# Attention, a gated MLP and a mixer block on one core: two weight chunks and one output-weight slab move between the first batch's v products

## The chip, the cores and the metric

The kernel runs on one core of one Trainium2 chip. The core has five engines that work side by side: TensorE (PE, matrix products), VectorE (DVE), ScalarE (ACT), GpSimd (POOL) and SyncE (SP), which here issues nearly all DMAs. Each engine works through its own instructions in order and waits on semaphores for the others. The metric is the device time of one execution in microseconds; the time of the kernel is the median of its runs.

## The reference

Four batches of 576 tokens, model width 512. Three blocks follow one another, all in float32:

```python
# 1. attention, 8 heads of 64, rotary embedding on q and k
attn = softmax(rotate(q) @ rotate(k).T / 8) @ v          # -> x [4, 576, 512]
# 2. spatial gating
h = gelu_tanh(x @ w_in);  u, v = h[..., :512], h[..., 512:]
v_n = (v - mean(v)) / sqrt(var(v) + 1e-6) * g_ln          # over the 512 features
v_s = einsum('ts,bsd->btd', w_sg, v_n) + b_sg             # over the 576 tokens
x = x + (u * v_s) @ w_out
# 3. mixer: low rank over the tokens (rank 32), then a channel MLP 512 -> 2048 -> 512
u = x + (x.transpose(0, 2, 1) @ U @ V).transpose(0, 2, 1)
out = u + maximum(u @ w_ch1, 0) @ w_ch2
```

The weights come in as 64-bit floats: they are loaded as pairs of 32-bit words, and the kernel makes 32-bit floats of them with integer steps on the chip.

## The kernel before, in words

The kernel has three stages. Attention (0 to about 295 us in the profile) is written out by hand. The gating stage (about 295 to 540) runs batch by batch, and the channel stage (from about 540) computes the last MLP for all tokens, with combined weight blocks.

In the gating stage the order on PE is the order of the code. On DVE, ACT, POOL and SP the program's planner places the instructions when the kernel is built, by readiness in its own model and by the order of the code; once placed, each engine keeps its order. `tc.issue_after(x)` holds the instructions traced inside it behind `x` on `x`'s engine.

The parts for a batch `b`, each float32 product made of products of high and low parts:

- `v_step(b, t)`: the v product of 128 tokens. At the end of a group of one or two `t`: GELU on ACT, mean and variance on DVE (L634, L635), epsilon added on POOL (L636), power -0.5 on POOL (L637), a small step on DVE (L640), the scaling on ACT (L641), and the high and low parts VH (ACT, L643) and VL (POOL, through `less`, L541). The last group, `t = 4`, holds the tails of two batches; its low parts are made on DVE (L648, L651), and L651 is marked in `LAST_D`.
- `u_step(b, k0)`: the u product with its GELU.
- `s_step(b, d)`: the product over the tokens (tile `m`) with the gate: L672 and L673 on DVE, then the parts GH (ACT) and GL (POOL). Four of them make a batch; the DVE gate L673 is marked in `LAST_G` and `LAST_D`.
- `o_step(b, e)`: the product with the output weights WOH and WOL (tile `w`), added to X on DVE (L691).
- `y_step`, `z_step`, `h_step`: the low rank mixer, with transposes, YH and YL (L712, L718), Z (L731, L732) and a last add to X (L740).
- `x_split(b)`: the parts XH (ACT, L429) and XL (POOL, L432) of the next batch.

PSUM holds four product tiles in rotation, so a product waits until the tile of the fourth before it has been read.

Beside this run the weights. `first_weights` makes 26 chunks of the channel stage's weights, one for each call of `chunk()`. A chunk is one ACT step (L775) and four DVE steps (L771 to L774) on 128x512; every second chunk adds four combine steps on DVE (L782 to L785) and a DMA of the result. It is traced inside `issue_after` for both entries of `LAST_D`, the last marked instruction on DVE and on ACT, as far as there are any. A call also issues the load of the next chunk, into one of two buffers. `other_weights` makes one slab of `w_out` for each `next(ow)`, four in all: an ACT step (L85), four DVE steps (L86 to L89), WOH on ACT (L573) and WOL on POOL. Chunks and slabs share the two buffers `cb`.

Before the change, batch 0 begins with its five v steps and four u steps; chunks 0 and 1 are called after the second and the fourth u step, when `LAST_D` holds L651. The first slab and `x_split(1)` are called behind `LASTS`, which are the last low parts of v on POOL (L644) and DVE (L648) and the last VH on ACT. The other three slabs follow the gates of batch 0, each behind its `LAST_G`.

Of the kernel before, what the change touches and what calls it, by code (L numbers as in the profile page):

```python
# [14 lines left out]
ALU = mybir.AluOpType  # L15
# [51 lines left out]
def tile_kernel(ctx: ExitStack, tc: tile.TileContext, qk, vv, tabs, w_in, g_ln, wsgT, b_sg, w_out, u_r, v_r, w1, w2, out):  # L67
    nc = tc.nc

    def f(ap):  # L70
        return ap.bitcast(F32)
# [8 lines left out]
    def from_f64(t, raw, clamp=nc.vector):  # L80

        lo, hi = raw[:, :, 0], raw[:, :, 1]
        tu = t.bitcast(U32)
        return (
            lambda: nc.scalar.activation(t, hi.bitcast(F32), AF.Abs),  # L85
            lambda: clamp.tensor_scalar(t, t, F64_LEAST, F64_MOST, ALU.max, ALU.min),  # L86
            lambda: nc.vector.tensor_scalar(tu, tu, 5, 2, ALU.logical_shift_left, ALU.logical_shift_right),
            lambda: nc.vector.scalar_tensor_tensor(tu, hi, 0xC0000000, tu, ALU.bitwise_and, ALU.bitwise_or),
            lambda: nc.vector.scalar_tensor_tensor(tu, lo, 29, tu, ALU.logical_shift_right, ALU.bitwise_or),  # L89
        )  # L90
# [326 lines left out]
    for h in range(2, NH):  # L417
        t = NC * h
# [104 lines left out]
    def ps_tile(name):  # L523
        return ps2.tile([P, 2, 512], F32, tag="ps", name=name)
# [15 lines left out]
    def less(out, a, b):  # L540
        return nc.gpsimd.tensor_tensor(out, a, b, ALU.subtract)  # L541
# [7 lines left out]
    def mark(x):  # L549
        LAST_D[0] = x  # L550
        return x
# [13 lines left out]
    def other_weights():  # L565
        for k in range(KT):
            tag = ("YH", "YL")[k % 2]
            raw = py.tile([P, 512, 2], U32, tag=tag, name=tag, bufs=2)
            t = p2.tile([P, 7, 256], F32, tag="cb", name="cb", bufs=2).rearrange("p a b -> p (a b)")[:, :512]
            nc.sync.dma_start(raw.rearrange("p n w -> p (n w)"), w_out[k * P:(k + 1) * P])  # L570
            for fn in from_f64(t, raw):
                fn()
            nc.scalar.activation(WOH[:, k], t, AF.Copy)  # L573
            less(WOL[:, k], t, f(WOH[:, k]))
            yield

    def gelu(t, ps):

        LAST_D[1] = nc.scalar.activation(t, ps, AF.Gelu_apprx_tanh)
        return t  # L580

    def mm3(ps, pairs, halves, first=True, last=True):
        n = len(pairs)
        for j, (l, r) in enumerate(pairs):
            for a in range(halves):
                rr = r[:, a * HALF:(a + 1) * HALF] if halves == 2 else r
                o = ps[:, a, :HALF] if halves == 2 else ps
                nc.tensor.matmul(o, l, rr, start=(first and j == 0), stop=(last and j == n - 1))  # L588

    def x_split(b):  # L590
        for k in range(KT):
            x_hi(b, k)
            x_lo(b, k)
# [15 lines left out]
    def v_step(b, t):  # L609

        if t == NC - 1 and b % 2:
            return
        pp = P
        first, last = next(g for g in (VG0 if b == 0 else VG) if g[0] <= t <= g[1])
        if t == first:
            VP[b] = ps_tile(f"v{b}_{t}")
        ps = VP[b]
        pr = []
        for k in range(KT):
            xh, xl = (TAILS[0][:, k], TAILS[1][:, k]) if t == NC - 1 else (x[:, k, t * P:(t + 1) * P] for x in (XH, XL))  # L620
            pr += [(xh, WVH[:, k]), (xh, WVL[:, k]), (xl, WVH[:, k])]
        mm3(ps[:pp, t - first, :], pr, 1)
        if t < last:
            return
        nt = last - first + 1
        slot[0] = 1024 - slot[0]
        hv = ug.rearrange("p a b -> p (a b)")[:, slot[0]:slot[0] + 1024].rearrange("p (a b) -> p a b", a=2)
        hv = (hv if b else py.tile([P, 2, DF], F32, tag="YL", name="YL", bufs=2))[:, :nt]
        gelu(hv, ps[:pp, :nt])
        st = p2.tile([P, 2, 6], F32, tag="bst", name="bst", bufs=2)  # L630
        mv = p2.tile([P, 2, 2], F32, tag="bmv", name="bmv", bufs=2)
        rs = p2.tile([P, 2], F32, tag="brs", name="brs", bufs=2)
        for j in range(nt):
            nc.vector.bn_stats(st[:pp, j], hv[:, j])  # L634
            nc.vector.bn_aggr(mv[:pp, j], st[:pp, j])  # L635
        nc.gpsimd.tensor_scalar(rs[:pp, :nt], mv[:pp, :nt, 1], 1e-6, None, ALU.add)  # L636
        nc.gpsimd.tensor_tensor(rs[:pp, :nt], rs[:pp, :nt], mhalf[:pp, :nt], ALU.pow)  # L637
        for j in range(nt):
            t = first + j
            nc.vector.scalar_tensor_tensor(mv[:pp, j, 1:], mv[:pp, j, :1], -1.0, rs[:pp, j:j + 1], ALU.mult, ALU.mult)  # L640
            nc.scalar.activation(hv[:, j], hv[:, j], AF.Identity, bias=mv[:pp, j, 1:], scale=rs[:pp, j:j + 1])  # L641
            if t < NC - 1:
                LASTS[2] = nc.scalar.activation(VH[:, t], hv[:, j], AF.Copy)  # L643
                LASTS[0] = less(VL[:, t], hv[:, j], f(VH[:, t]))  # L644
            else:
                a, z = hv[:D, j], hv[D:, j]
                LASTS[2] = nc.scalar.activation(VH[:D, t], a, AF.Copy)
                LASTS[1] = nc.vector.tensor_tensor(VH[D:, t], a, f(VH[:D, t]), ALU.subtract)  # L648
                nc.scalar.activation(VT[D:], z, AF.Copy)
                nc.scalar.activation(VT[:D], z, AF.Copy)  # L650
                mark(nc.vector.tensor_tensor(VT[D:], z, f(VT[D:]), ALU.subtract))  # L651

    def u_step(b, k0):
        ps = ps_tile(f"u{b}_{k0}")
        pr = []
        for k in range(KT):
            wh, wl = WUH[:, k, k0 * P:(k0 + 1) * P], WUL[:, k, k0 * P:(k0 + 1) * P]
            pr += [(wh, XH[:, k]), (wh, XL[:, k]), (wl, XH[:, k])]
        mm3(ps, pr, 2)
        LAST_D[1] = nc.scalar.activation(h2(ug[:, k0]), ps[:, :, :HALF], AF.Gelu_apprx_tanh)  # L660
# [456 lines left out]
    fw = first_weights()  # L1117
    next(fw)
    chunk = lambda: next(fw, None)
    for t in range(NC):  # L1120
        v_step(0, t)
    RB[NP - 1] = p2.tile([P, S], F32, tag="g", name="g", bufs=2)
    for t in sorted(due):
        for fn in due.pop(t):
            fn()
    for k0 in range(KT):
        u_step(0, k0)
        if k0 % 2:
            chunk()
    ow = other_weights()  # L1130
    with ExitStack() as es:
        for x in LASTS:
            es.enter_context(tc.issue_after(x.ins))
        next(ow)
        x_split(1)
    for b in range(B - 1):
        n = b + 1
        for d in range(KT):
            if d == 1 and n > 1:
                x_split(n)  # L1140
            s_step(b, d)
            if b == 0:
                with ExitStack() as es:
                    es.enter_context(tc.issue_after(LAST_G[0].ins))
                    next(ow, None)
            if b == 1:
                if d < 2:
                    run(h_step, b - 1, 2 * d, 2 * d + 1)
                if d % 2:
                    chunk()  # L1150
            if b == 2 and d % 2 == 0:
                chunk()
        run(v_step, n, 0, 1)
        chunk()
        if b == 0:
            run(v_step, n, 2, 3)
            chunk()
        for e in range(2):
            o_step(b, e, 0, KT - 1)
        chunk()  # L1160
        for e in range(2):
            o_step(b, e, KT - 1)
        o_step(b, 2)
        chunk()
        o_step(b, 3)
        if b > 0:
            if n % 2 == 0:
                x_tail(n)
            v_step(n, 2)
            chunk()  # L1170
            run(v_step, n, 3, 4)
            if n == 3:
                chunk()
        if n == 1:
            u_step(n, 0)
            chunk()
            u_step(n, 1)
            run(y_step, b, 0, 2)
            u_step(n, 2)
            run(z_step, b, *range(NC - 1))  # L1180
            y_step(b, 4)
            u_step(n, 3)
            z_step(b, 4)
            chunk()
        elif n == 2:
            run(y_step, b, 0, 2)
            u_step(n, 0)
            chunk()
            run(z_step, b, *range(NC - 1))
            y_step(b, 4)  # L1190
            u_step(n, 1)
            z_step(b, 4)
            u_step(n, 2)
            chunk()
            run(h_step, b, 0, 1)
            u_step(n, 3)
            run(h_step, b, 2, 3)
        else:
            for k0 in range(KT):
                u_step(n, k0)  # L1200
                if k0 % 2:
                    chunk()
    a, b = B - 2, B - 1
# [103 lines left out]
```

## Time and profile before

| what | value |
|---|---|
| median of 3 runs | 914.27 us (913.6 to 918.02) |
| the profiled execution | 912.03 us, of which its span is 910.2 us |
| PE busy | 885.3 us (97% of the span) |
| DVE busy | 738.8 us (81%) |
| ACT busy | 464.7 us (51%) |
| POOL busy | 401.9 us (44%) |
| mean granted clock of PE | 0.996 |

Busy times come from one profiled execution. The span runs from the first to the last instruction; the execution's time lies around it. A view by stretch gives the busy time of each engine in a window; a timeline gives single instructions with the idle time before them and what ended it, in square brackets; a view of waits sums the idle time of an engine by what ended it. In section 4 of the page, the chain that ended last is PE for 65% of the span and DVE for 21%.

### The profile page before, as it was taken

How to read it: one execution, taken by the hardware profiler on the slowest of the kernel's cores; microseconds unless marked ns; L12 is line 12 of the kernel's file. 1: busy time of each engine (PE TensorE's matmuls, PEld its weight loads, DVE VectorE, ACT ScalarE, POOL GpSimd, SP SyncE). 2: the span in 40 equal slices, each digit the busy share in tenths (PEclk: the TensorE clock that was granted, in tenths of full speed). 3: DMA queues.
4: the chain of work that ended last, by engine and by line, in shares of the span. 5: the costliest groups of instructions: out<-in, count | busy, mean ns of one | idle time of the engine just before them, and what ended most of it. 6: DMA issues, size and time to landing. Idle time of an engine off the chain costs nothing.

```text
span 910.2 us, 14331 instructions
## 1 busy us (share of the span) xinstructions
PE 885.3 (97%) x5279; PEld 802.9 (88%) x5279; DVE 738.8 (81%) x991; ACT 464.7 (51%) x719; POOL 401.9 (44%) x302
## 2 busy tenths in 40 slices
PE   8999999999999998889999999999999999999998
PEld 4677878878877897789999988999999999999997
DVE  6677798898998487889799897789889876897557
ACT  4556666666667454433624356554655455544222
POOL 6997778778727455242443333442100110141010
PEclk9999999999999999999999999999999999999999
DMA  6788777687662531525245348968589378647821
GB/s 192 206 193 203 186 203 190 166 213 187 152 170 63 158 107 51 174 86 174 89 150 175 99 143 278 317 240 299 197 277 397 141 247 299 239 126 247 296 86 70
DMA packets 101330, 170.36 MB, mean 187 GB/s; under 512 B 32822, under 2 KB 50508, under 8 KB 101260
## 3 DMA queue, kind: packets, MB, share of 16 engines
q1 hardware_dynamic: 100960, 169.36, 60.3%
q8 instruction: 42, 0.69, 0.3%
q14 instruction: 28, 0.23, 0.1%
q10 hardware_dynamic: 300, 0.08, 0.0%
HBM read 110.07 MB, written 41.49 MB: 167 GB/s over the span
## 4 chain that ended last, share of the span: by engine, by line
PE 65%; DVE 21%; DMA 4%; ACT 4%; issue 4%; POOL 2%; SPq 0%; DVEq 0%; POOLq 0%; ACTq 0%
PE pv L278 12%; PE st L251 8%; PE sm L209 4%; DVE cb L773 2%; PE v L588 2%; PE w L588 1%; PE u L588 1%; DVE cb L774 1%; DVE cb L771 1%; DVE MX L214 1%; PE m L588 1%; DVE cb L772 1%; PE a2X L907 1%; PE r2x L907 1%; PE a4X L907 1%
## 5 line engine op out<-in xcount | busy, mean ns | idle before, releaser
L214 DVE TENSOR_REDUCE MX<-sm 128x1 f32<-128x576 f32 (+1 forms) x160 | 117.0, 747 | 36.4 <-PE sm L209 31.1
L278 PE MATMUL pv<-pc,VV 128*65 128x288 f32 (+1 forms) x516 | 145.7, 405 | 0.0
L251 PE MATMUL st<-Q,K 65*128 65x288 f32 (+3 forms) x640 | 126.3, 320 | 2.1 <-ACT pc L254 0.8
L251 PEld LDWEIGHTS st<-Q,K 65*128 65x128 f32 (+3 forms) x640 | 95.0, 178 | 16.7 <-DVE MX L214 1.8
L254 ACT ACTIVATE pc<-st 128x576 f32<-128x576 f32 x129 | 83.1, 645 | 31.0 <-PE st L251 28.6
L278 PEld LDWEIGHTS pv<-pc,VV 128*65 128x65 f32 (+1 forms) x516 | 69.3, 136 | 29.1 <-issue 0.2
L831 POOL TENSOR_TENSOR r1l<-t,r1h 128x768 fp32r<-128x768 f32 x12 | 23.0, 1915 | 156.5 <-ACT r1h L828 140.6
L831 POOL TENSOR_TENSOR r7l<-tmp,r7h 128x768 fp32r<-128x768 f32 x12 | 25.6, 2130 | 116.9 <-ACT r7h L828 85.8
L209 PE MATMUL sm<-K,Q 128*128 128x288 f32 (+1 forms) x320 | 72.0, 315 | 2.1 <-ACT pc L254 0.6
L173 POOL TENSOR_TENSOR Q<-raw,Q 128x576 fp32r<-128x576 f32 x30 | 45.7, 1523 | 29.6 <-ACT Q L168 29.5
L209 PEld LDWEIGHTS sm<-K,Q 128*128 128x128 f32 (+1 forms) x320 | 50.0, 178 | 8.5 <-DVE MX L214 1.3
L154 POOL TENSOR_TENSOR raw<-raw,tab 128x576 f32<-128x576 f32 x31 | 50.6, 1631 | 2.4 <-DMA raw<-in_qk 2.4
L588 PE MATMUL u<-XH,setA 128*128 128x288 f32 x256 | 47.2, 302 | 1.9 <-DVE X L691 1.9
L331 DVE TENSOR_TENSOR X<-stage,rb 64x576 f32<-64x576 f32 x30 | 47.5, 1586 | 1.5 <-DMA rb<-rr 1.0
L156 POOL TENSOR_TENSOR raw<-raw 128x576 f32<-128x576 f32 x31 | 47.6, 1536 | 0.5
L541 POOL TENSOR_TENSOR GL<-g,GH 128x576 fp32r<-128x576 f32 x16 | 26.3, 1651 | 45.6 <-ACT GH L674 45.6
L155 POOL TENSOR_TENSOR raw<-raw,tab 128x576 f32<-128x576 f32 x31 | 44.4, 1433 | 0.0
L588 PEld LDWEIGHTS u<-XH,setA 128*128 128x128 f32 x256 | 39.2, 194 | 2.3 <-DVE X L691 2.1
L588 PE MATMUL v<-setA,XH 128*128 128x512 f32 x128 | 39.6, 391 | 0.0
L294 ACT ACTIVATE stage<-pv 65x576 f32<-65x576 f32 x31 | 20.0, 647 | 29.7 <-PE pv L278 29.6
L775 ACT ACTIVATE cb<-raw 128x512 f32<-128x512 f32 x26 | 17.4, 671 | 34.3 <-DMA raw<-in_w 28.8
L258 ACT ACTIVATE pt<-st 64x576 f32<-64x576 f32 x31 | 19.9, 643 | 27.7 <-PE st L251 27.6
(1149 smaller groups left out, 2494.4 us busy)
## 6 DMA issues: line engine op xcount, KB each, us to landing
raw<-in_qk SPq DMA_DIRECT2D x31, 576.0 KB
combo<-cb SPq DMA_DIRECT2D x16, 896.0 KB
YH<-combo SPq DMA_DIRECT2D x27, 512.0 KB
raw<-in_w SPq DMA_DIRECT2D x26, 512.0 KB
K<-Q SPq DMA_DIRECT2D x30, 288.0 KB
YL<-combo SPq DMA_DIRECT2D x15, 512.0 KB
u<-setA SPq DMA_DIRECT2D x16, 384.0 KB
w2l<-lows SPq DMA_DIRECT2D x12, 512.0 KB
```

Source lines behind the costliest of these rows:

```text
L154: lambda: e.tensor_tensor(raw[:, 0], raw[:, 0], tab[:, 0], ALU.mult),
L155: lambda: e.tensor_tensor(raw[:, 1], raw[:, 1], tab[:, 1], ALU.mult),
L156: lambda: e.tensor_tensor(raw[:, 0], raw[:, 0], raw[:, 1], ALU.add),
L173: nc.gpsimd.tensor_tensor(Q2[:, :S], rot, f(Q1), ALU.subtract)
L209: nc.tensor.matmul(ps[:TS[t], n, :HALF], Q1[:, t * P:t * P + TS[t]], K1[:, n * HALF:(n + 1) * HALF], start=True, stop=True)
L214: nc.vector.tensor_reduce(MXs[h % 2][:TS[t], t:t + 1], ps[:TS[t], :, :HALF], AX.XY, ALU.max)
L251: nc.tensor.matmul(ps[:kk, n, :HALF], l[:, c * P:c * P + kk], r[:, ns], start=st, stop=not st)
L254: nc.scalar.activation(h2(pc[:kk]), ps[:kk, :, :HALF], AF.Exp, scale=0.125)
L278: nc.tensor.matmul(o, l, r, start=(c == 0 and j == 0), stop=(c == NC - 1 and j == len(pr) - 1))
L331: nc.vector.tensor_tensor(X[b][rows, pr], STAGE.pop(h - 1 + a)[:D], RB[i][:, a], ALU.mult)
L588: nc.tensor.matmul(o, l, rr, start=(first and j == 0), stop=(last and j == n - 1))
L831: return e.tensor_tensor(out, a, b, ALU.subtract)
```

## The change

Chunks 0 and 1 are called between the v steps of batch 0, after `t = 1` and `t = 3`. The first slab of `w_out` is called after the first u step, without a hold. Batch 0 calls two chunks behind its gates `d = 1` and `d = 3`, and no longer one after `o_step(b, 2)` and one after `z_step(b, 4)`. Batch 1 calls three chunks at its gates in place of two. Batch 3's only call finds no chunk left. The epsilon of the variance is added on DVE.

```diff
@@ -633,7 +633,7 @@
         for j in range(nt):
             nc.vector.bn_stats(st[:pp, j], hv[:, j])
             nc.vector.bn_aggr(mv[:pp, j], st[:pp, j])
-        nc.gpsimd.tensor_scalar(rs[:pp, :nt], mv[:pp, :nt, 1], 1e-6, None, ALU.add)
+        nc.vector.tensor_scalar(rs[:pp, :nt], mv[:pp, :nt, 1], 1e-6, None, ALU.add)
         nc.gpsimd.tensor_tensor(rs[:pp, :nt], rs[:pp, :nt], mhalf[:pp, :nt], ALU.pow)
         for j in range(nt):
             t = first + j
@@ -1117,21 +1117,22 @@
     fw = first_weights()
     next(fw)
     chunk = lambda: next(fw, None)
+    ow = other_weights()
     for t in range(NC):
         v_step(0, t)
+        if t in (1, 3):
+            chunk()
     RB[NP - 1] = p2.tile([P, S], F32, tag="g", name="g", bufs=2)
     for t in sorted(due):
         for fn in due.pop(t):
             fn()
     for k0 in range(KT):
         u_step(0, k0)
-        if k0 % 2:
-            chunk()
-    ow = other_weights()
+        if k0 == 0:
+            next(ow)
     with ExitStack() as es:
         for x in LASTS:
             es.enter_context(tc.issue_after(x.ins))
-        next(ow)
         x_split(1)
     for b in range(B - 1):
         n = b + 1
@@ -1143,10 +1144,12 @@
                 with ExitStack() as es:
                     es.enter_context(tc.issue_after(LAST_G[0].ins))
                     next(ow, None)
+                if d % 2:
+                    chunk()
             if b == 1:
                 if d < 2:
                     run(h_step, b - 1, 2 * d, 2 * d + 1)
-                if d % 2:
+                if d > 0:
                     chunk()
             if b == 2 and d % 2 == 0:
                 chunk()
@@ -1161,7 +1164,8 @@
         for e in range(2):
             o_step(b, e, KT - 1)
         o_step(b, 2)
-        chunk()
+        if b > 0:
+            chunk()
         o_step(b, 3)
         if b > 0:
             if n % 2 == 0:
@@ -1181,7 +1185,6 @@
             y_step(b, 4)
             u_step(n, 3)
             z_step(b, 4)
-            chunk()
         elif n == 2:
             run(y_step, b, 0, 2)
             u_step(n, 0)
```

## Rows read from the trace of the kernel before

**Rows 1.** Busy time by stretch: window, length, busy time per engine (instructions), clock, DMA.
```profile
305.00:323.00 18.00, 18.00 (x124) 17.15 (x123) 5.00 (x15) 12.00 (x19) 11.26 (x14) 1.00 0.56 166
348.00:396.00 48.00, 39.28 (x256) 36.93 (x256) 36.80 (x61) 21.56 (x35) 20.95 (x18) 0.93 0.29 94
396.00:448.00 52.00, 52.00 (x347) 49.01 (x346) 45.43 (x81) 20.85 (x31) 14.92 (x14) 1.00 0.45 145
448.00:522.00 74.00, 74.00 (x520) 71.65 (x520) 66.56 (x103) 28.61 (x42) 31.06 (x21) 1.00 0.41 132
```

**Rows 2.** Waits of PE, 348 to 396: total us, times, longest.
```profile
PE q L588 <- DVE Z L732: 2.5, 1, 2.5
PE u L588 <- DVE X L691: 1.9, 1, 1.9
PE z L728 <- DVE YL L718: 1.5, 1, 1.5
PE w L588 <- ACT WOH L573: 1.1, 1, 1.1
PE w L588 <- ACT ug L579: 0.9, 1, 0.9
PE w L588 <- POOL WOL L541: 0.8, 1, 0.8
```

**Rows 3.** Timeline of PE behind the first waits: start, length, instruction.
```profile
353.26 0.69 PE L588 MATMUL w<-GH,WOH 128*128 128x288 f32 x2
...
356.31 0.42 PE L588 MATMUL w<-GH,WOL 128*128 128x288 f32 x2
```

**Rows 4.** Timeline of DVE, 318 to 428.
```profile
318.13 0.16 DVE L640 SCALAR_TENSOR_TENSOR bmv<-bmv,brs 128x1 f32<-128x1 f32 x1 [0.99 <-POOL brs L637]
322.46 0.69 DVE L648 TENSOR_TENSOR VH<-YL,VH 64x512 fp32r<-64x512 f32 x1 [4.17 <-ACT VH L647]
...
323.89 0.43 DVE L771 TENSOR_SCALAR cb<-cb 128x512 f32<-128x512 f32 x1
...
326.09 1.93 DVE L88 SCALAR_TENSOR_TENSOR cb<-YH,cb 128x512 uint32<-128x512 uint32 x1
...
336.18 0.82 DVE L672 SCALAR_TENSOR_TENSOR g<-m,small,bh 128x576 f32<-128x576 f32 x1
...
338.70 0.43 DVE L785 TENSOR_TENSOR cb<-cb 128x256 f32<-128x256 f32 x1
...
343.07 0.69 DVE L89 SCALAR_TENSOR_TENSOR cb<-YL,cb 128x512 uint32<-128x512 uint32 x1
...
392.59 1.77 DVE L773 SCALAR_TENSOR_TENSOR cb<-raw,cb 128x512 uint32<-128x512 uint32 x1
394.38 0.69 DVE L732 TENSOR_TENSOR Z<-z,Z 32x512 fp32r<-32x512 f32 x1
...
427.62 0.75 DVE L691 TENSOR_TENSOR X<-w,X 128x576 f32<-128x576 f32 x1
```

**Rows 5.** Timeline of PE at two places that read DVE's results.
```profile
325.26 0.69 PE L588 MATMUL m<-WST,VH 128*128 128x288 f32 x4
325.80 0.56 PE L588 MATMUL m<-WS,VH 128*128 128x288 f32 x3
...
434.03 0.38 PE L710 MATMUL t<-ident,X 128*128 128x128 f32 x2
```

**Rows 6.** Timeline of GpSimd, 315 to 333.
```profile
315.76 0.23 POOL L636 TENSOR_SCALAR brs<-bmv 128x2 f32<-128x2 f32 x1 [0.88 <-DVE bmv L635]
...
325.63 7.35 POOL L432 TENSOR_TENSOR XL<-X,XH 128x576 fp32r<-128x576 f32 x4 [3.41 <-ACT XH L429]
```

**Rows 7.** Busy time while the first weights land, columns as in rows 1.
```profile
305.00:310.00 5.00, 5.00 (x25) 4.15 (x24) 1.03 (x3) 3.08 (x5) 4.07 (x6) 1.00 0.99 291
```

**Rows 8.** Waits of PE, 522 to 570.
```profile
PE w L588 <- POOL GL L541: 0.9, 1, 0.9
PE z L728 <- DVE YH L714: 0.7, 1, 0.7
```

## Prediction

> **What bounds the kernel now.** I read the busy time by stretch first [rows 1]. TensorE (PE) works without a gap from 396 to 522 us, but in 348 to 396 it works 39.28 of 48 us, so 8.7 us are idle, and the mean granted clock is 0.93. The same view shows the odd thing: in 305 to 323 VectorE (DVE) is busy for 5.00 of 18 us, in 348 to 396 for 36.80 of 48. So DVE is nearly empty just before the stretch in which PE starves, and full in it. The waits of PE name the releasers [rows 2]: 1.1 and 0.8 us for a slab of the output weights (WOH, WOL), 0.9 for the GELU that frees a product's PSUM tile, 1.9 for a residual add (X L691), 1.5 for YL, 2.5 for Z; together 8.7. The clock: after the first waits a pair of matmuls takes 0.69 us, later 0.42 [rows 3]. A mean of 0.93 over 48 us, with levels of 1.2 and 2.4 GHz, means 6.7 us at the lower one, which costs at most 3.4 us of work; by the pairs it is 6.7 x (0.69 - 0.42) / 0.69 = 2.6. I take 3.0. So the stretch holds 8.7 + 3.0 = 11.7 us to be had.
>
> Then the order on DVE [rows 4]. The last small step of batch 0's v chain is at 318.13; after it DVE waits 4.17 us for ScalarE, makes the low parts of v's tail (L648 is the first), and at 323.89 the first weight chunk begins. From there to 339.13 stand chunks c0 and c1, the first output slab and, in their midst, one gate (L672 at 336.18, 0.82, with its product about 1.6 together). That is 15.2 - 1.6 = 13.6 us of weights, while the first gate's products were done on PE at 325.8, when the next gate's begin [rows 5]. All that PE waits for after 348 comes behind this on DVE. The chunks start at 323.89 because the code holds their DVE steps behind the last DVE instruction marked before them, the last low part of the v tail, and the output slab stands behind the same low parts.
>
> **Part 1, two chunks between the v products.** At the new place (after v steps 1 and 3) no DVE instruction has been marked yet, so only a GELU on ScalarE holds them. They are 4 + 4 conversion steps and 4 combine steps. Undisturbed, a conversion's two one-input steps take 0.43 each, its two two-input steps 0.69 each (L89 at 343.07), a combine step 0.43 (L785) [rows 4]: 2.24 a conversion. c0, c1 and the slab are 3 x 2.24 + 4 x 0.43 = 8.4 us undisturbed; in the trace they took 13.6, as L88 shows: 1.93 beside the XL work of GpSimd, 7.35 us long [rows 4, 6].
>
> How much idle time can they use? Not all 13.0 of the 18 us: their weights come first. The DMA engines are full (0.99, 291 GB/s) from 305 to 310 [rows 7], and up to the end of the first chunk there are 1.4 MB to land by the tiles' sizes, so by an estimate it is there at 305 + 1.4 / 0.29 = 309.8 us. From then to 323.9 are 14.1 us; DVE uses 5.00 - 1.03 = 4.0 of them [rows 1, 7] and about 0.7 for L648: 9.4 us are free for 8.4. It fits if undisturbed.
>
> **Part 2, the output slab,** behind the first u product: its four DVE steps are in that sum; two ScalarE steps and the low part on GpSimd move too. ScalarE is busy 12.00 of 18 us there and GpSimd 11.26 [rows 1]: room in both, at no cost while the v chain has the room named below. SP issues no more than before: the loads are the same, those of chunks 2 and 3 start earlier as their buffers come free earlier, behind the loads of w_out that were issued with the first.
>
> The rule that speaks against it: measured, a two-input step takes 1.93 us beside GpSimd and 0.69 without [rows 4]. The Trainium skill, GPSIMD Engine Reference, section Specifications, says that GpSimd shares its SBUF interfaces with VectorE, with contention for instructions of two inputs and in two-port modes. The trace agrees; by that rule the moved steps are stretched again wherever GpSimd works, 63% of the time there, and stretch the low parts of v in turn: 8.4 + 0.63 x (13.6 - 8.4) = 11.7 us, more than the 9.4 free.
>
> What PE would notice: L648 ends at 323.15, and PE comes to the matmuls that read it at 325.26 [rows 4, 5]: 2.1 us of room. The moved steps stand in one line with the chain on DVE. Bounds of the chain's delay: 0 (all in gaps) and 13.6 - 9.4 + one long step of 1.93 = 6.1. Less the room, PE waits 0 to 4.0 us, plus up to 1.5 for a fallen clock (half of the 3.0 above). I take +1.0, near the row without contention. Below zero it can't go: PE does not wait here now.
>
> **Part 3, behind the gates.** Chunks 2 and 3 now stand behind the second and the fourth gate of batch 0; the two later ones (after o step 2 and behind z) go. The batch keeps six chunks and loses the 13.6 us of parts 1 and 2. So DVE comes to the last slabs up to 13.6 us earlier, where PE wants them 2 us earlier: the waits of 1.1 and 0.8 go. The gates free the GELU's buffer earlier by the same: the 0.9 goes. X L691 (1.9) has less before it: gone. The Z step at 394.38 stands behind a step of 1.77 of a chunk, at 392.59 [rows 4], and that is the chunk taken from there: the 2.5 goes. YL's 1.5 is partly a chain of its own, two copies on ScalarE and two steps on DVE against one u product: I leave 0.5 of it, and 0.5 for the rest. With the clock back, -11.7 + 1.0 = -10.7; bounds -11.7, and -4.5 if only the first three waits (2.8) and 1.7 of the clock go.
>
> Batch 1 gets one chunk more at its gates, 2.2 us alone and up to 4 x 1.93 = 7.7 beside GpSimd. The next that PE needs behind it are the transposes at 434.03; the residual add that they read begins at 427.62 and takes 0.75 [rows 4, 5]: 5.7 us of room. I take 0, by the row without contention; bounds 0 and +2. Batch 2 keeps nine chunks. Batch 3 loses its only one, 2.24 + 4 x 0.43 = 4.0 us between its gates, and PE waits there 0.9 for GL and 0.7 for YH [rows 8]: bounds 0 and -1.6; I take -0.8, the middle.
>
> **Part 4, epsilon on VectorE.** Eleven adds of 0.23 leave GpSimd [rows 6]; the nearest row of DVE is L640 with 0.16 [rows 4]. Each chain is 0.07 shorter, or longer by up to 1.93 if a moved step comes between. PE waits for no v chain but by the 0.9 above, so I count 0, with +0.16 x 11 = 1.8 of DVE time as the upper bound.
>
> **Sum**, against the profiled execution's own 912.03 us (span 910.2 and 1.8 around it): +1.0 - 10.7 + 0 - 0.8 + 0 = -10.5. The median of the runs, 914.27, is 2.2 above that execution; I set the difference against the median: 903.8, say **904**.
>
> **The rivals.** (a) Half of it: only what hangs on the slabs and gates goes (-4.5); X, Z and YL are late by chains of their own. 914.3 - 4.5 = 909.8. For: Z and YL pass three engines. Against: a chunk's step stands right ahead of Z on DVE [rows 4].
> (b) Slower: the idle time cannot be used, as DVE works its line in order. It is idle while its next instruction waits for GpSimd or ScalarE (4.17 us at L648); if the moved steps wait at the head of that line for their weights, or stand ahead of the chain's, the low part is late by up to 13.6: PE waits 13.6 - 2.1 = 11.5 at 325 and runs slowly after it, 13.0 with the 1.5. DVE is then no longer behind after 348, which gives back 4.5 to 11.7: from +1.3 to +8.5, the middle +4.9: 919.2. It decides from a delay of 5 us on if 4.5 comes back, of 12 if all does. For: full DMA to 310. Against: 9.4 us free for 8.4.
> (c) It does not do what it says: the planner may place the chunks behind the chain all the same. 914. Against: what kept them back is the hold, and that falls.
>
> **How the numbers follow.** Forecast 0.58 (900 to 907.5, or below), (a) 0.20 (907.5 to 912), (b) 0.15, (c) 0.07. A measurement of this kernel tells 0.5%, or 4.6 us, from no change: 909.7 to 918.8 is the same. Half of (a) is faster, half the same; (b) is slower with 0.11, the same with 0.04; (c) the same. So faster 0.68, same 0.21, slower 0.11. The range leaves out 0.13 above, most of (b), and 0.07 below 900, where all the bounds fall well: 900 to 914.5.
>
> **What would show it.** Right: L771 to L774 and L782 to L785 on DVE before 323; the first gate (L672) near 326 instead of 336; no wait of PE above 0.5 us in what is now 348 to 396, with a clock near 1.00; the same work of PE behind it, about 10 us earlier. Wrong: a wait of PE near 325 for VH or VL above 1 us; waits for Z or X that stay; a new wait in batch 1 behind its three gate chunks; or a gain at 396 that is lost again by 570.

## The result, and the profile after

The changed kernel takes 904.55 us (median of 10 runs, 903.1 to 914.04) against 914.94 (10 runs, 912.34 to 918.02) for the kernel before: a ratio of 0.9901, 95% interval 0.9871 to 0.993. The forecast was 904. Its profiled execution took 904.36 us with a span of 902.6, 7.7 less than the 912.03 of the profile before.

So the total was right. The terms of the sum were not all right, and this is what the trace after is good for. The first view is the busy time by stretch, columns as in [rows 1]; the stretches lie up to 8 us earlier than before.

```profile
305.00:323.00 18.00, 18.00 (x124) 17.11 (x123) 12.06 (x35) 10.61 (x17) 8.84 (x9) 1.00 0.70 216
340.00:388.00 48.00, 44.36 (x281) 41.01 (x280) 40.69 (x70) 23.04 (x36) 18.86 (x15) 0.96 0.38 124
```

DVE was busy for 5.00 of 18 us before 323; now it is for 12.06. That is what the change set out to fill. In the 48 us behind, PE's idle time fell from 8.7 to 3.6 us, and the clock is 0.96 instead of 0.93. The 3.6 us that are left, and a new loss ahead of 340, have names in the waits of PE (total us, times, longest), 300 to 388, after:

```profile
PE u L588 <- DVE X L691: 2.8, 1, 2.8
PE m L588 <- POOL VL L541: 1.2, 2, 0.6
PE w L588 <- POOL WOL L541: 0.8, 1, 0.8
PE m L588 <- ACT VH L643: 0.7, 1, 0.7
```

Against [rows 2]: the waits for Z, YL, WOH and the GELU are gone, WOL's 0.8 stands as it was, X L691's has grown from 1.9 to 2.8, and the products of batch 0's gates (m) now wait 1.9 for VH and VL, where PE did not wait at all.

Waits leave out what a fallen clock costs. So I measured how long PE takes from the first matmul of one stage to the first of the next; a stage's length holds its waits and its clock. Each number below is the difference of two start times in PE's timeline (us); the letters are the tiles that PE writes. "Again" are second profiles of the same two kernels, taken later on another chip.

```
stage, from its first matmul to the next's  before  again   after  again   after-before  forecast
gates of batch 0 (m to v of batch 1)         14.96  14.94   17.52  17.16      +2.6          +1.0
v of batch 1                                 11.02  10.99   10.93  10.92      -0.1           0
o products of batch 0 (w to u)               20.04  19.86   17.22  17.38      -2.8       \
u of batch 1, transposes (u to z)            12.92  12.76   12.79  12.86      -0.1        | -10.7
z of batch 0, rest of u (to m of batch 1)     7.69   7.83    5.81   5.75      -1.9        |
first gate of batch 1, q (m to m)             7.04   7.34    4.27   4.26      -2.8       /
then to z of batch 2, in batch 3's gates    124.42 125.65  124.43 124.41       0.0           0
from there to the last w of batch 3           9.51   9.54    7.32   7.31      -2.2          -0.8
to the second product V,Z into r0y           28.86  28.90   28.85  29.25       0.0           0
sum                                         236.46 237.81  229.14 229.30      -7.3         -10.5
```

The four stages of part 3 gave 7.6 us, not 10.7; the gates cost 2.6, not 1.0; batch 3 gave 2.2, not 0.8. In sum the profiled executions differ by 7.3 in these stages and 0.35 outside them. Up to the first u product of batch 1 (the first three rows) only 0.35 us is won: PE begins it at 367.90, before at 368.11. What the o products give back, the gates have taken before; nearly all of the gain lies behind that point.

**The moved steps.** The timeline after, all engines, shows them at the new place (start, us, engine, line, operation; in brackets idle before and releaser).

```profile
310.40 0.67 ACT L775 ACTIVATE cb<-raw 128x512 f32<-128x512 f32 x1 [1.23 <-DMA raw<-in_w]
311.10 0.43 DVE L771 TENSOR_SCALAR cb<-cb 128x512 f32<-128x512 f32 x1 [2.95 <-ACT cb L775]
...
314.56 0.76 DVE L334 TENSOR_TENSOR X<-X,g 128x576 f32<-128x576 f32 x1 [1.11 <-DMA g<-rr]
315.23 1.28 DVE L634 BATCH_NORM_STATS2 bst<-YL 128x6 f32<-128x512 f32 x2
...
318.57 0.14 DVE L636 TENSOR_SCALAR brs<-bmv 128x2 f32<-128x2 f32 x1
318.62 0.69 DVE L773 SCALAR_TENSOR_TENSOR cb<-raw,cb 128x512 uint32<-128x512 uint32 x1
318.86 2.12 POOL L637 TENSOR_TENSOR brs<-brs,small 128x2 f32<-128x2 f32 x2 [4.26 <-DVE brs L636]
...
319.88 0.69 DVE L774 SCALAR_TENSOR_TENSOR cb<-raw,cb 128x512 uint32<-128x512 uint32 x1
320.51 0.23 DVE L640 SCALAR_TENSOR_TENSOR bmv<-bmv,brs 128x1 f32<-128x1 f32 x2
...
320.76 1.53 ACT L641 ACTIVATE YL<-YL,bmv,brs 128x512 f32<-128x512 f32 x2 [4.59 <-DVE bmv L640]
...
322.58 0.42 DVE L785 TENSOR_TENSOR cb<-cb 128x256 f32<-128x256 f32 x1
...
325.65 0.82 DVE L648 TENSOR_TENSOR VH<-YL,VH 64x512 fp32r<-64x512 f32 x1 [2.65 <-ACT VH L647]
...
328.25 0.80 SPq L570 DMA_DIRECT2D YL<-in_w_out  x2
...
328.76 0.82 DVE L672 SCALAR_TENSOR_TENSOR g<-m,small,bh 128x576 f32<-128x576 f32 x1 [0.60 <-PE m L588]
```

First, ScalarE waits 1.23 us for the first chunk's DMA and starts at 310.40; the estimate was 309.8. Second, the sixteen DVE steps of two chunks and a slab run from 311.10 to 323.00 at 0.40 to 0.69 us each, 8.4 in sum, as if alone. Third, the v chain is late: the statistics of v 2 and 3 (L634) start at 315.23, behind L334, a multiplication of the attention's end that waits for a DMA; L636 stands between steps of the chunk and the slab; and ScalarE's normalization (L641) starts at 320.76. The same instructions before:

```profile
312.17 1.29 DVE L634 BATCH_NORM_STATS2 bst<-YL 128x6 f32<-128x512 f32 x2 [0.35 <-ACT YL L579]
...
314.76 0.76 DVE L334 TENSOR_TENSOR X<-X,g 128x576 f32<-128x576 f32 x1 [1.30 <-DMA g<-rr]
...
317.01 0.81 ACT L641 ACTIVATE YL<-YL,bmv,brs 128x512 f32<-128x512 f32 x1 [1.50 <-DVE bmv L640]
...
322.25 0.33 SPq L570 DMA_DIRECT2D YL<-in_w_out  x1
...
349.54 0.69 DVE L89 SCALAR_TENSOR_TENSOR cb<-YH,cb 128x512 uint32<-128x512 uint32 x1
...
353.83 0.69 DVE L89 SCALAR_TENSOR_TENSOR cb<-YL,cb 128x512 uint32<-128x512 uint32 x1
```

L634 stood ahead of L334 there. It is 3.06 us later now, L641 3.75, L648 3.19 (322.46 before [rows 4]). The first gate L672 stands at 328.76 instead of 336.18, 7.4 us earlier.

**What did not come.** The next output slabs. The loads of the second and the fourth reuse buffers (YL) that v's low parts free, so they are issued from 328.25 on, when the last low part ends (L651, 326.50 + 1.66), instead of from 322.25. DVE after, up to the wait for X L691 and behind it:

```profile
332.97 0.43 DVE L86 TENSOR_SCALAR cb<-cb 128x512 f32<-128x512 f32 x1 [2.60 <-ACT cb L85]
...
343.96 0.68 DVE L89 SCALAR_TENSOR_TENSOR cb<-YH,cb 128x512 uint32<-128x512 uint32 x1
...
354.16 0.68 DVE L89 SCALAR_TENSOR_TENSOR cb<-YL,cb 128x512 uint32<-128x512 uint32 x1
...
362.81 1.50 DVE L771 TENSOR_SCALAR cb<-cb 128x512 f32<-128x512 f32 x1
...
364.38 1.34 DVE L772 TENSOR_SCALAR cb<-cb 128x512 uint32<-128x512 uint32 x1
...
367.09 0.75 DVE L691 TENSOR_TENSOR X<-w,X 128x576 f32<-128x576 f32 x1
...
379.11 1.22 DVE L718 TENSOR_TENSOR YL<-t,YH 128x1024 fp32r<-128x1024 f32 x1
...
389.33 0.69 DVE L732 TENSOR_TENSOR Z<-z,Z 32x512 fp32r<-32x512 f32 x1 [4.75 <-ACT Z L731]
```

DVE waits 2.60 us at 332.97 for ScalarE's step L85, which waits for the load. The third slab's last step ended at 350.23 before and ends at 344.64: 5.6 us earlier, not "up to 13.6". The fourth slab's ended at 354.52 before and ends at 354.84: not earlier at all, since steps of the two gate chunks stand among the slab's on DVE. So the wait for its WOL, 0.8, stays. L691 follows four steps of a chunk, of which L771 and L772 take 1.50 and 1.34 instead of 0.43 beside this subtraction on GpSimd, which makes the low parts of v:

```profile
362.73 2.72 POOL L541 TENSOR_TENSOR VL<-ug,VH 128x512 fp32r<-128x512 f32 x2 [3.82 <-ACT VH L643]
```

L691 starts at 367.09; before it was 367.31. PE's last w product ends at 365.07, and its next product waits until L691 is done:

```profile
367.90 0.85 PE L588 MATMUL u<-XH,setA 128*128 128x288 f32 x2 [2.83 <-DVE X L691]
```

Z, on the other hand, has nothing ahead of it on DVE any more (4.75 us idle before it), as forecast.

### The profile page after: what moved, and what is told of

Its sections match the earlier page's. It is cut to its first block, busy times and chain, and to the rows that moved or that the text cites. A ratio compares the mean times of both kernels' runs of the same rounds, so it can differ in the third digit from the quotient of the medians.

```text
span 902.6 us, 14348 instructions
## 1 busy us (share of the span) xinstructions
PE 883.5 (98%) x5279; PEld 801.6 (89%) x5279; DVE 733.1 (81%) x1002; ACT 465.2 (52%) x719; POOL 395.2 (44%) x291
## 4 chain that ended last, share of the span: by engine, by line
PE 79%; DVE 10%; issue 3%; POOL 3%; ACT 2%; DMA 2%; SPq 0%; DVEq 0%; POOLq 0%; ACTq 0%
PE pv L278 13%; PE st L251 8%; PE m L588 5%; PE u L588 4%; PE w L588 4%; PE sm L209 4%; PE v L588 3%; DVE MX L214 1%; PE r5x L907 1%; PE a2X L907 1%; PE a4X L907 1%; PE a5X L907 1%; PE a8X L907 1%; PE r4x L907 1%; PE a11X L907 1%
## 5 line engine op out<-in xcount | busy, mean ns | idle before, releaser
L588 PE MATMUL m<-WS,VH 128*128 128x288 f32 x192 | 33.5, 297 | 0.7 <-ACT VH L643 0.7
```

## The experiments

The theory: the gain is DVE work of the weights that leaves 324 to 395; the gates are late because the v chain shares DVE's line with it; what is left behind 340 is the amount of DVE work. Rivals: the gain hangs on a single step, such as the chunk behind z; the moved steps are stretched by GpSimd; epsilon is what delays the gates; the remaining wait is one of order, which another place for a chunk would cure. Every ratio is to the kernel before, run beside it on the same chip.

**Epsilon alone**, on the kernel before:
```
-nc.gpsimd.tensor_scalar(rs[:pp, :nt], mv[:pp, :nt, 1], 1e-6, None, ALU.add)
+nc.vector.tensor_scalar(rs[:pp, :nt], mv[:pp, :nt, 1], 1e-6, None, ALU.add)
```


> The kernel before with only the epsilon added on VectorE. Both theories: the same time within 1.5 us, since PE waits for no v chain but by the 0.9 us of its GELU; each chain's hand-over from the variance to the power is some 0.1 us shorter. A rival (the epsilon alone gives a good part of the 10 us, because the GELU waits for the chain): 2 us or more faster, the PE wait for the GELU gone.


Measured: 918.67 us, ratio 1.0036 [1.0015, 1.0058]: slower. Waits of PE, 300 to 392, in its profile:
```profile
...
PE w L588 <- ACT WOH L573: 2.0, 2, 1.0
PE w L588 <- POOL WOL L541: 1.8, 2, 1.0
...
PE v L588 <- DVE g L672: 1.6, 1, 1.6
```
Neither expectation held. The adds take 0.16 us each, eleven of them 1.7 in all, too little for the 3.3 us. What else differs is the order of DVE's line, which the planner made anew with the add in it:
```profile
314.61 0.76 DVE L334 TENSOR_TENSOR X<-X,g 128x576 f32<-128x576 f32 x1 [3.69 <-DMA g<-rr]
315.29 1.28 DVE L634 BATCH_NORM_STATS2 bst<-YL 128x6 f32<-128x512 f32 x2
```
The statistics of v 2 and 3 now stand behind L334 and its DMA and start at 315.29 instead of 312.17, though nothing else was changed. DVE waits 3.69 us there with their input at hand. L641 comes at 318.65 instead of 317.01, the gates take 16.85 us instead of 14.96 and the o products 21.83 instead of 20.04. All profiles of kernels with epsilon on DVE show L634 behind L334 (seven kernels here, the changed one among them), all those with it on GpSimd ahead of it (the kernel before, and four more below). So the order goes with the epsilon; that it makes the 3.3 us is argued, since no run has the add on DVE in the old order.

**The two early chunks alone**, on the kernel before (epsilon on GpSimd, the slab at its old place):
```
     for t in range(NC):
         v_step(0, t)
+        if t in (1, 3):
+            chunk()
...
         u_step(0, k0)
-        if k0 % 2:
-            chunk()
```


> The kernel before with only this: chunks 0 and 1 called after v steps 1 and 3 of batch 0 and no longer in its u steps; slab, epsilon and all later calls as before. Theory 1 (the prediction's: the early slots drain VectorE's line, and that takes the later waits away): 7 to 11 us faster than before, waits for X L691 and Z mostly gone. Theory 2 (formed from the trace after: the early slots cost at the gates what they save at the output slabs, and the gain comes from the two places that lose a chunk later, ahead of Z in batch 0 and in batch 3's gates): within 3 us of before; PE reaches the first o step later than before by 1 to 3 us, the wait for Z of 2.5 us stays, and the waits for GL and YH in batch 3 stay.


Measured: 909.87 us, ratio 0.9945 [0.9927, 0.9962], some 5 us, between the two expectations. The gates take 14.92 us, the same as before: two chunks between the v products cost PE nothing. The o products are 3.4 us shorter (16.67). The later waits stay, as the waits of PE show:
```profile
PE q L588 <- DVE Z L732: 2.5, 1, 2.5
PE u L588 <- DVE X L691: 1.9, 1, 1.9
PE z L728 <- DVE YL L718: 1.3, 1, 1.3
```

**The later places alone**: the kernel before with only part 3.
```
+                if d % 2:            # behind two gates of batch 0
+                    chunk()
...
-                if d % 2:            # b == 1
+                if d > 0:
...
         o_step(b, 2)
-        chunk()
+        if b > 0:
+            chunk()
...
             z_step(b, 4)
-            chunk()
```


> The changed kernel with chunks 0 and 1 and the first output slab put back to their old places, and the epsilon on GpSimd; the later calls (two chunks behind batch 0's gates, none after o step 2 and behind z, three in batch 1, none in batch 3) as in the changed kernel. Theory 1: VectorE has the old block of 13.6 us and the two gate chunks ahead of the slabs, so PE's waits in the o steps grow by 3 us or more; 0 to 6 us slower than before. Theory 2: the waits for Z, YL (about 4.6 together) and in batch 3 (about 2) go all the same; 3 to 7 us faster than before by the later part, less what the slabs lose.


Measured: 910.73 us, ratio 0.9953 [0.9934, 0.9972].
```profile
PE w L588 <- ACT WOH L573: 5.6, 2, 4.6
PE w L588 <- POOL WOL L541: 1.6, 2, 0.8
```
Without the early chunks PE waits 5.6 us for slabs (o products 24.28), but Z's 2.5 and X's 1.9 are gone and batch 3 gives its 2.2. The two halves multiply to 0.9945 x 0.9953 = 0.9898, the ratio of the whole: the gain doesn't hang on a single step. Neither half holds the slab's early place or epsilon. Together those two can't be told from nothing here, with intervals that leave some 3 to 4 us to either side.

**Batch 3's chunk put back**, on the changed kernel: batch 1 gives its extra chunk up, and the last one falls to batch 3 again.
```
-                if d > 0:
+                if d % 2:
                     chunk()
```


> The changed kernel, but batch 1 calls two chunks at its gates as before, so that the last chunk falls again between batch 3's gates. Theory 2 (and the ledger of the two traces: 2.1 us were won between 522 and 530): about 2 us slower than the changed kernel, the waits for GL (0.9) and YH (0.7) back. Theory 1 as predicted: 0.8 us slower. If batch 1's third chunk had a price, this kernel would be faster than the changed one.


Measured: 908.36 us, 0.9935 [0.9915, 0.9955]. Batch 3's stage is 9.16 us again instead of 7.32, and the waits of [rows 8] return in its profile:
```profile
PE z L728 <- DVE YH L714: 0.7, 1, 0.7
PE w L588 <- POOL GL L541: 0.6, 1, 0.6
```
So the term is 1.8 us of PE's time here, and batch 1's third chunk costs nothing (124.41 us without it, 124.43 with it). The ratios differ by more, 3.3 us (0.9935 against 0.9899 to 0.9901). The profile puts the rest at places that this edit doesn't touch: u to z took 1.3 longer, and the gates of batch 0 19.27, 1.75 longer, at a granted clock of 0.91 in that stretch, where the changed kernel's first profile has 1.00 (the same in one more run, held, below).

**The output slab put back** behind the hold, on the changed kernel:
```
         u_step(0, k0)
-        if k0 == 0:
-            next(ow)
...
             es.enter_context(tc.issue_after(x.ins))
+        next(ow)
         x_split(1)
```


> The changed kernel with the first output slab back behind the last low parts of v. Theory 3 (from the two halves run alone: the early chunks gain 3.4 us in the o steps and cost nothing at the gates, the later calls lose 4.2 there and gain 6 later, so it is the slab that costs 2.5 at the gates and saves 3.7 in the o steps): the waits for VH and VL at the first gates (1.9) go or fall below 0.8, the waits for WOH and WOL in the o steps rise to 3 us or more; in sum 0 to 3 us slower than the changed kernel. Rival (the chunks among the v steps delay the gates, the slab does not): the waits at the gates stay at 1.5 to 2.5 us.


Measured: 905.10 us, 0.9902 [0.988, 0.9923]. The gates take 14.91 us, without a wait, though L634 stands behind L334 here too (315.24): the chain comes earlier than in the changed kernel (L641 at 319.54 instead of 320.76, L648 at 323.90 instead of 325.65), and PE's room covers what is left of the delay. The o products are 20.46 instead of 17.22, with these waits:
```profile
PE w L588 <- ACT WOH L573: 3.2, 1, 3.2
PE u L588 <- DVE X L691: 1.2, 1, 1.2
```
What the slab costs at the gates it gives back behind them; the total doesn't move.

**Epsilon put back on GpSimd**, on the changed kernel: the first diff reversed.


> The changed kernel with the epsilon on GpSimd. Alone, the epsilon made the kernel before 0.36% slower, by another order on VectorE and not by its own 0.15 us. Theory 3: in the changed kernel it is worth under 1.5 us either way. Rival (the add on VectorE stands behind chunk steps there and so makes the v chain and the gates late): the waits for VH and VL at the first gates go, and the kernel is 1.5 to 4 us faster than the changed one.


Measured: 903.51 us, 0.9888 [0.986, 0.9916]. L634 is ahead of L334 again, at 311.72. The wait for VH goes and those for VL fall from 1.2 to 0.4. The gates take 16.15 us instead of 17.52, the stages together 228.33 instead of 229.14. The intervals overlap with the changed kernel's, so a gain of about 1 us is what the profile shows and the times don't resolve. So two delays add up at the gates. With the slab alone they lose 1.2 us (16.15 for 14.96), with epsilon's order and the chunks nothing (14.91), with both 2.6: by these numbers PE has a room of some 2 us there, and it is spent once.

**The chunk behind z put back**, one of the two at batch 0's gates given for it:
```
-                if d % 2:            # b == 0
+                if d == 3:
                     chunk()
...
             z_step(b, 4)
+            chunk()
```


> The changed kernel with batch 0's chunk behind the second gate taken away and the one behind the z step put back, the count of chunks in the batch the same. If the chunk's steps ahead of Z on VectorE made the wait of 2.5 us, it comes back (2 to 3 us), and YL's with it in part; against it, the o steps have one chunk less before them: the wait for WOL (0.8) and that for X L691 (2.8, and a fallen clock behind it) shrink. In sum within 3 us of the changed kernel. If Z was late for another reason, no wait for Z, and 2 us faster or more.


Measured: 906.32 us, 0.9924 [0.9895, 0.9953]. DVE's timeline has the pair of [rows 4] again, and PE its wait for Z, 2.5 us:
```profile
390.82 1.77 DVE L773 SCALAR_TENSOR_TENSOR cb<-raw,cb 128x512 uint32<-128x512 uint32 x1
392.61 0.69 DVE L732 TENSOR_TENSOR Z<-z,Z 32x512 fp32r<-32x512 f32 x1
```
So the chunk ahead of Z was the cause of that wait. X L691 still waits 3.2 us here, against the expectation, although one chunk fewer stands ahead of it: four steps of a chunk still stand directly before it on DVE (L771 at 361.69 to L774 at 365.36, L691 at 366.30). (The profiled execution, 910.09 us, is the slowest of the four.)

**Another order at the second o product**: the chunk behind `run(v_step, n, 2, 3)`, v products of the next batch, put behind `o_step(b, 2)` instead.
```
 run(v_step, n, 2, 3)
-chunk()
...
 o_step(b, 2)
-if b > 0:
-    chunk()
+chunk()
```


> The changed kernel with batch 0's chunk after v steps 2 and 3 moved behind o step 2. In the changed kernel's trace that chunk's steps and its combine stand on VectorE ahead of the two residual adds that the next u product waits for (2.8 us, then a fallen clock). Theory (VectorE's order decides, not its amount of work): that wait goes, 3 to 4.5 us faster than the changed kernel. Rival (VectorE has too much to do in this stretch, whatever the order): the wait moves to the transposes or to YL and Z, and the time is within 1.5 us of the changed kernel.


Measured: 904.37 us, 0.9896 [0.9872, 0.9921]; the wait for X stays at 2.8. It tells nothing apart: the planner filled the place with the next chunk, and DVE's order around L691 came out as it was.

**All chunks of that stretch behind the residual adds** (one behind each of the o steps 2 and 3, none before them), then the same with epsilon on GpSimd:
```
 run(v_step, n, 2, 3)
-chunk()
...
-chunk()                              # between the first o steps
+if b > 0:
+    chunk()
 o_step(b, 2)
-if b > 0:
-    chunk()
+chunk()
 o_step(b, 3)
+if b == 0:
+    chunk()
```


> The changed kernel, but batch 0's chunks after v steps 2 and 3 and between the o steps are called after o step 2 and o step 3 instead, so that both are held behind residual adds on VectorE; no chunk's steps stand ahead of the first two adds any more. (Moving a single call by one step had left VectorE's order there as it was, and PE's wait of 2.8 us too.) Order theory: the wait for X L691 falls from 2.8 us below 1, with the fallen clock behind it; the stretch from the first o step to the second u product of batch 1 falls from 17.2 to about 14.5 us, and the later ones grow by under 1; 2 to 4 us faster than the changed kernel. Amount theory: VectorE comes late to YL or Z instead, and the sum of the stretches up to batch 1's gates stays within 1 us.

> The same with the epsilon back on GpSimd. By the ledgers so far (epsilon back: first gates 16.15 us instead of 17.52, the rest the same) and the order theory: 1 to 1.5 us faster than the held kernel, so 3 to 5 us faster than the changed one and the fastest of all; PE's wait for VH at the first gates gone. If the two do not add: the same as the better of the two alone.


Measured: 905.12 us, 0.9906 [0.9891, 0.992], and 904.68, 0.9908 [0.9892, 0.9925]. The 2 to 5 us that the order theory expected didn't come. X's wait is gone in both. In the first, PE works through 340 to 375, and the o products take 12.95 us, 4.3 less than in the changed kernel; in the second, where waits for the slab stay, they take 15.12. But YL's wait is back (2.8 at the longest with epsilon on GpSimd, too); of the first of the two, the wait, the stretch behind (columns as in [rows 1]), and DVE:
```profile
PE z L728 <- DVE YL L718: 2.7, 1, 2.7
```
```profile
340.00:375.00 35.00, 35.00 (x233) 32.93 (x232) 32.85 (x60) 15.66 (x24) 14.42 (x11) 1.00 0.26 87
370.00:384.00 14.00, 11.32 (x68) 10.03 (x67) 10.72 (x20) 4.51 (x7) 1.58 (x1) 0.81 0.73 241
```
```profile
378.21 1.22 DVE L718 TENSOR_TENSOR YL<-t,YH 128x1024 fp32r<-128x1024 f32 x1
```
L718 comes at 378.21, 0.9 us earlier than in the changed kernel, while PE gets to its reader 4.3 earlier. The stage of z takes 11.39 us instead of 5.81: -4.3 for the o products, -1.5 for u to z and +5.6 here come to -0.2. (All stages take 230.80 instead of 229.14, since the gates of batch 0 took 18.98; on that more below.) The wait moved along and nothing was won. X's wait is thus one of order: it goes when the chunk directly ahead of L691 goes. YL's speaks for the amount of work: the same six chunks stand ahead of L718, DVE has no idle time from 366.17 to the end of L718, and it is busy for 32.85 of the 35 us, 33.45 in the changed kernel. But of the 5.6 us only 2.7 are the wait; the other 2.9 go with the clock, which fell behind it. So it is shown that this other order of the same chunks made the kernel no faster (905.12 and 904.68, beside 904.42 for the changed kernel). That the amount alone is the limit is argued: no run has fewer chunks ahead of YL and none directly ahead of L691.

**Both kernels once more**, beside these:


> The changed kernel once more, beside the two held ones on one chip: 0.988 to 0.992 of before. Its profile: the first gates 17.5 us, the wait for X L691 2.8, as in the first profile, since each engine's order is fixed; what may differ is the granted clock behind the waits.

> The kernel before, profiled a second time. Its first profiled execution was 912.0 us against a median of 915; the change was worth 7.6 us between the profiled executions and about 9 in the ratio. If the difference is the clock: the same waits of PE as in the first profile, and more time at the lower clock, 1 to 4 us slower. If it is the waits (for a DMA): a wait that the first profile does not have.


Measured: 904.42 us, 0.9899 [0.9881, 0.9916], and 913.89, 1.0006 [0.9989, 1.0023]. Their profiles stand in the table above. The changed kernel's has the same waits at the same places, but for the one on VH (0.3 instead of 0.7). That of the kernel before has a second wait for WOL and one of 1.0 for X at the transposes, which the first lacks; the stages that hold them are no longer for it (19.86 for 20.04, 12.76 for 12.92).

## Why the prediction was right, and where its steps failed

**Part 1, the room on DVE: right.** 8.4 us of steps fitted into the stretch at their undisturbed lengths, and the early chunks alone left the gates at 14.92 us. The price by contention, 11.7, did not come: most of the moved steps meet GpSimd idle (4.26 us of it in one piece) or at work on 128x2 tensors. Where it works on a 128x512 tensor, steps are stretched (1.50 and 1.34 instead of 0.43). The Trainium skill, GPSIMD Engine Reference, section Specifications, which the prediction weighed, names contention on the SBUF interfaces that GpSimd shares with VectorE, for instructions with two inputs and in two-port modes. This trace agrees for two inputs where GpSimd works on a large tensor beside the step (L88 at 335.00 takes 1.80 instead of 0.69); whether the one-input steps run in such a mode no run here shows. What failed was my estimate of the price by GpSimd's mean busy share, the 11.7.

**Part 2, the gates' wait: right in kind, the term mis-sized.** +1.0 was forecast, +2.6 came. The chunks cost nothing; the slab does, since its steps lie where v 2 to 4 are normalized, and so does epsilon, by the order that comes with it. I had named L648 as the late part; PE waited instead for VH and VL of v 2 and 3, made by ScalarE and GpSimd earlier in the chain, and L648 was done (326.47) when PE came to it (328.03). This is rival (b)'s mechanism, at a fraction of its size: L648 was 3.2 us late, and (b) decides from 5.

**Part 3, the failed step.** "So DVE comes to the last slabs up to 13.6 us earlier" and "X L691 (1.9) has less before it: gone". The third slab came 5.6 us earlier, the fourth 0.3 later, as two loads wait for buffers that the delayed v tail frees and the gate chunks stand in line with the slabs. X's wait grew to 2.8 with a fallen clock behind it: L691 came only 0.2 us earlier than before. These stages gave 7.6 us, not 10.7. I had counted DVE work as removed that stays in the batch: two of its six chunks now stand behind the gates, where DVE is just as full. The step on Z was right (2.8 of 2.5, with the clock), YL's too (1.9 where 1.0 was forecast).

**Batch 1: right.** Its extra chunk costs 0.0 in 124.4 us. **Batch 3: mis-sized**, -2.2 for -0.8: both waits went whole, and 0.6 us more that the waits don't show. With DVE's only extra work gone, the far bound was the one to take, not the middle. **Epsilon: the step failed, the term held.** I priced the add, 0.07 us a chain less, and it is that short. Alone the move cost 0.36%, by all signs through the order of DVE's line. In the changed kernel, where other waits end last, no run tells its price from 0.

**The signs.** Two of those that I had named for being wrong came: PE waits for VH and VL at the gates (1.9 us in all, none longer than 0.7), and the wait for X stayed. The first gate stands at 328.76, not near 326.

**The total.** That 904 came to within 1 us is luck in part. The profiles differ by 7.7 and 7.2 us (the stages of the table by 7.3 and 8.5), the medians by some 9 (0.9899 to 0.9901 of 914). Part of the gap between the two is the clock. The same wait for Z was followed by a full clock in the first profile of the kernel before and by 0.83 in the second, which cost 1.2 us in the next stage (125.65 against 124.42); the changed kernel has no wait there. Before again:

```profile
390.00:400.00 10.00, 7.47 (x45) 7.23 (x44) 8.64 (x12) 1.69 (x4) 2.96 (x2) 0.83 0.17 52
```

The gates' new wait does the same. In the run held, where the gates' waits are 1.2 and 0.7 us as in the changed kernel, the clock fell behind them, and the stage took 18.98 us instead of 17.52. The stretch in held, then after:

```profile
322.20:341.00 18.80, 16.92 (x113) 16.22 (x112) 13.19 (x15) 11.24 (x21) 13.23 (x9) 0.91 0.37 130
```
```profile
322.20:341.00 18.80, 16.95 (x120) 16.04 (x119) 12.66 (x15) 11.39 (x21) 13.57 (x10) 1.00 0.37 129
```

PE is as busy in both and does 113 instructions instead of 120. The remaining 1 us or so is not settled; single executions of one kernel on one chip lay 3 to 4 us apart (911.68 to 915.86, 902.5 to 905.81). Thus 904 came out from two terms that were too good and one that was too poor, and from setting them against a median of three runs, while the profile that they were read from ran 2.9 us under the median of ten. With the stages as measured, -7.3, the same sum would have said 907.

## What to carry to other kernels

An engine's idle time ahead of a starved stretch can be used for work of that stretch, but price it for each step by what stands in line with it at that very place: two chunks were free there, and a slab a few us later cost 1.2 to 2.6. A step is only earlier by as much as its load is, so follow the buffer that the load needs. After any edit, however small, compare the order of each engine's line: here, with one add of 0.16 us moved, a chain came to stand behind a step that waits for a DMA. When a wait goes, ask whether the engine behind it has less work or only another order; with 33 of 35 us busy, another order only moved the wait.

## What the runs showed of the hardware

A one-input DVE step on 128x512 (0.43 us) is stretched as well as a two-input one when GpSimd works on a 128x512 tensor beside it, to 1.34 to 1.50 here, while two-input steps beside a 128x2 power on GpSimd kept their 0.69. And one and the same wait was followed by a full clock in one execution and a fallen one in another (levels 2.4 and 1.2 GHz): 1.00 and 0.83 behind Z's 2.5 us, 1.00 and 0.91 behind the gates' 1.9. A wait's price in one profile may lack the clock's part: 1.2 and 1.5 us in these two, 2.9 behind YL's wait in the run held.
